# Two more late Q tiles, additions for z tied to VectorE's normalises, and a new list of steps

## The chip, the cores and the metric

The kernel runs on one core of a Trainium2 chip. The metric is the device time of one execution in microseconds; before the change it is 510.95 us, the median of three runs (510.87 to 511.24).

## The reference

One block of a transformer on 2048 tokens of width 576, in bfloat16. A layernorm feeds two branches in parallel, linear attention with 32 heads of 18, and a gated feed-forward of width 4608:

```python
def _A_ref(x, wqkv, wo):
    q, k, v = split_heads(x @ wqkv)
    phi = lambda t: jnp.where(t > 0, t + 1, jnp.exp(t)) + 1e-6
    pq, pk = phi(q), phi(k)
    kv = jnp.einsum("bhsd,bhse->bhde", pk, v)
    z = jnp.einsum("bhsd->bhd", pk)
    num = jnp.einsum("bhqd,bhde->bhqe", pq, kv)
    den = jnp.einsum("bhqd,bhd->bhq", pq, z)[..., None] + 1e-6
    return merge_heads(num / den) @ wo
def _B_ref(x, w_gate, w_up, w_down):
    return (_gelu(x @ w_gate) * (x @ w_up)) @ w_down
xn = _layernorm(x)
return x + _A_ref(xn, A_wqkv, A_wo) + _B_ref(xn, B_w_gate, B_w_up, B_w_down)
```

## The kernel before

The tokens are 16 tiles (n = 0 to 15) of 128. There is a head, which does the layernorm and gathers the attention's sums, and then four groups (sc = 0 to 3) of four tiles each, which do the feed-forward and the output.

**The head.** For each tile: statistics of two halves and their aggregate on VectorE (L226, L229); the reciprocal deviation as a logarithm and an exponential on ScalarE (L233, L234); the normalised tile `xn`, on VectorE (L247) where the string NORM has a D for the tile, on ScalarE (L242) where it has an A, and then GpSimd first makes its bias (L237); the transposed copy `xnT`, by TensorE and copies (L268, L272) for tiles 0 and 1, by a DMA transpose that SyncE issues (L275) for the others. K is multiplied in two halves of 288 columns with five matmuls each (L283), one PSUM bank for each half, so a half can't be multiplied for the next tile until phi has read this tile's. Phi is an exponential on ScalarE (L298) and a maximum on VectorE (L303). Q goes the same way through two other banks. G = xn^T phi(k) is accumulated in PSUM over the tiles (L322, seven matmuls a tile now, two more a tile at the head's end, and a strip, L329); V is multiplied in only afterwards (L402). The sum z of phi(k) over the tiles is added up on GpSimd, one addition of 128 x 576 a tile from tile 1 on (L212), and read by a matmul near the head's end (L390).

**Late Q.** The tiles in LATE have no Q in the head. Their Q is computed at the start of the group they lie in, in front of its gate/up (`late_q`, with the class `_LateQ`): per tile ten and then eight matmuls on 64 rows, which take two row tiles of TensorE in turn (L353, the line that gate/up's matmuls have too), then an exponential (L714), a minimum (L715) and a maximum with an addition (L716) for each of two halves. Two such tiles are held at a time, with two banks each, out of a ring of eight that the gate/up units and the output tiles use as well. Before, group 1 has late tiles 6 and 7, group 2 has 9, 10 and 11, group 3 has 13, 14 and 15, and group 0 none.

**The groups.** Gate/up: 18 pairs of units of 18 half-row matmuls with 512 columns for each of two F tiles (L353, 648 matmuls a group), gelu on ScalarE (L694), product on VectorE (L695). Then down and the attention's part for the four tiles (L800, L805), the sum with x (L814), and the store. Weights are loaded by SyncE as buffers come free.

**What sets the order.** In the head every piece of work is a step with an engine, a planned cost, a rank and the steps that it comes after. The order in which the steps are emitted, and so the order on each engine's queue, is written out in the text HEAD; a step that HEAD lacks would be placed by the planner `in_order` behind it. Engines take their instructions strictly in this order, and wait by semaphores for the data and buffers that they need. The letters: x load of x, s statistics, a aggregate, r reciprocal deviation, b bias on GpSimd, n normalise, t transpose on TensorE, c the copy or DMA into `xnT`, m multiply, e exponential, p phi, z addition for z, G accumulation of G, w five idle matmuls, B mask, g clearing of buffers. The numbers are tile, then 1 for K or 0 for Q, then half. The planned costs and tails (`took`, `tail`, `ready`) have no effect while HEAD names every step. A step's `after` alone makes no semaphore: it only orders.

Of the kernel before, what the change touches and what calls it, by code (L numbers as in the profile page):

```python
# [43 lines left out]
LATE = (6, 7, 9, 10, 11, 13, 14, 15)  # L44
# [16 lines left out]
def kernel(  # L61
# [149 lines left out]
    def z_add(n):
        nc.gpsimd.tensor_tensor(  # L212
            out=z_bf[:] if n == NS - 1 else z_sum[:], in0=pk[:, 0, PK0:PK0 + D] if n == 1 else z_sum[:], in1=pk[:, n, PK0:PK0 + D],
            op=ALU.add,
        )

# [29 lines left out]
    def ln_norm(n, c0=0, c1=D):  # L246
        nc.vector.tensor_scalar(  # L247
# [91 lines left out]
    SYNC = mybir.DependencyInfo(mybir.DependencyClass.Sync, mybir.DependencyReason.DATA)  # L339
# [130 lines left out]
    for n0 in range(8, NS, 2):  # L470
        step(("x", n0), "SP", 1.30, n0 - 5.5, [], lambda n0=n0: load_x(n0, 2), ready=1.6 * n0 + 2.0, tail=3.0)
    for n in range(NS):
        lead = LEAD[n] if n < 4 else 0.0
        after_x = [("x", n // 2 * 2)] if n >= 8 else []
# [58 lines left out]
    def in_order(steps):  # L533
# [351 lines left out]
```

## Time and profile before

| | before |
|---|---|
| median of three runs | 510.95 us |
| span of the profiled execution | 509.1 us |
| TensorE busy | 504.4 us, 4553 matmuls |
| VectorE, ScalarE, GpSimd busy | 215.7, 143.3, 26.6 us |
| head, until the first gate/up matmul | 56.6 us |
| last K multiply of the head ends | 46.6 us |
| addition for z on GpSimd (L212) | 1.29 us mean |
| DMA transpose (L275) | 1.21 us of issue, 2.6 us to landing (median) |

The profile is one execution. The busy share tells which engine is full; the chain of waits is followed back from the last instruction, and names at each piece what was being waited for; the timeline has every instruction with its start, its length and, in brackets, how long its engine had stood in front of it and what released it. A TensorE that is busy says nothing of the pace of its matmuls; the starts of successive ones do.

### The profile page before, as it was taken

Reading aid. Unit: us, or ns where it says so; the run is one execution under the profiler, and the core shown is the slowest. Engines: PE = TensorE matmul, PEld = TensorE weight load, DVE = VectorE, ACT = ScalarE, POOL = GpSimd, SP = SyncE. Lnnn points to the kernel's source line nnn. Section 1 sums busy time; section 2 is a strip of 40 time slices with the busy share of each in tenths; the row PEclk is TensorE's granted clock in tenths of the full one; section 3 lists DMA queues with packets and bytes.
Section 4 is the critical chain, followed back from the end, with each engine's and each line's share of the span. In section 5 each row is a group of like instructions: output and inputs, shape, how many; then the busy total and the mean of one; then the engine's idle time right before and its main releaser. Section 6 shows DMA issues by size and latency. Waiting matters only on the chain.

```text
span 509.1 us, 10828 instructions
## 1 busy us (share of the span) xinstructions
PE 504.4 (99%) x4553; PEld 303.5 (60%) x4553; DVE 215.7 (42%) x465; ACT 143.3 (28%) x273; POOL 26.6 (5%) x40
## 2 busy tenths in 40 slices
PE   8999999999999999999999999999999999999997
PEld 7878644444877544444777544445777444445774
DVE  7994555555100465455000655554101556544101
ACT  6886233223300332333000423323000433232000
POOL 3556000000000000000000000000000000000000
PEclk9999999999999999999999999999999999999999
DMA  6556599999020455666000465576000565551000
GB/s 211 135 102 163 155 262 283 253 267 234 18 71 0 117 155 163 170 160 153 14 13 0 125 170 164 153 171 136 13 13 0 147 172 154 163 130 14 13 13 23
DMA packets 119850, 62.00 MB, mean 122 GB/s; under 512 B 25778, under 2 KB 119098, under 8 KB 119802
## 3 DMA queue, kind: packets, MB, share of 16 engines
q1 hardware_dynamic: 119658, 61.17, 46.6%
q8 instruction: 35, 0.57, 0.5%
q14 instruction: 13, 0.11, 0.1%
q10 hardware_dynamic: 144, 0.15, 0.1%
HBM read 53.60 MB, written 2.36 MB: 110 GB/s over the span
## 4 chain that ended last, share of the span: by engine, by line
PE 97%; DVE 1%; DMA 0%; ACT 0%; issue 0%
PE ps_all L353 57%; PE ps_all L800 28%; PE ps_all L283 5%; PE ps_all L805 3%; PE ps_all L322 3%; DMA x_sb<-in_A_x_dram 0%; PE ps_all L788 0%; PE ps_all L329 0%; DVE stats L226 0%; DVE xn L247 0%; PE ps_all L402 0%; PE ps_all L291 0%; PE ps_all L740 0%; PE ps_all L268 0%; ACT phi_e L298 0%
## 5 line engine op out<-in xcount | busy, mean ns | idle before, releaser
L353 PE MATMUL ps_all<-xnT,wg 64*128 64x512 bf16 x1152 | 272.1, 376 | 0.0
L353 PE MATMUL ps_all<-xnT,wu 64*128 64x512 bf16 x1152 | 271.6, 376 | 0.0
L695 DVE TENSOR_TENSOR hT<-ps_all,gl 128x512 bf16<-128x512 f32 x144 | 99.6, 692 | 125.9 <-ACT gl L694 125.8
L353 PEld LDWEIGHTS <-wu 64*128 64x128 bf16 x1152 | 108.3, 94 | 68.0
L353 PEld LDWEIGHTS <-wg 64*128 64x128 bf16 x1152 | 108.3, 94 | 67.6
L800 PE MATMUL ps_all<-wd_sb,hT 128*128 128x288 bf16 (+2 forms) x1152 | 147.1, 286 | 0.0
L694 ACT ACTIVATE gl<-ps_all 128x512 f32<-128x512 f32 x144 | 86.0, 597 | 186.3 <-PE ps_all L353 186.1
L800 PEld LDWEIGHTS <-hT 128*128 128x128 bf16 x1152 | 110.9, 98 | 30.9 <-issue 1.2
L814 DVE TENSOR_TENSOR res<-ps_all,x_sb 128x288 bf16<-128x288 f32 (+2 forms) x32 | 13.8, 454 | 146.3 <-PE ps_all L805 88.1
L353 PE MATMUL ps_all<-xnT,wr 64*128 64x512 bf16 x288 | 54.7, 376 | 0.0
L714 ACT ACTIVATE gl<-ps_all 128x288 f32<-128x288 f32 x16 | 5.9, 410 | 119.0 <-PE ps_all L353 117.8
L283 PE MATMUL ps_all<-wqkv_sb,xnT 128*128 128x288 bf16 x230 | 30.9, 286 | 0.5 <-DVE hT L303 0.4
L283 PEld LDWEIGHTS <-xnT 128*128 128x128 bf16 x230 | 21.8, 97 | 6.0 <-issue 0.6
L298 ACT ACTIVATE phi_e<-ps_all,neg 128x288 f32<-128x288 f32 x48 | 23.1, 496 | 4.8 <-PE ps_all L283 2.0
L353 PEld LDWEIGHTS <-wr 64*128 64x128 bf16 x288 | 14.0, 94 | 16.7
L805 PE MATMUL ps_all<-m_sb,pqT 128*128 128x288 bf16 (+2 forms) x128 | 20.9, 286 | 0.0
L322 PE MATMUL ps_all<-hT,xn 128*128 128x288 bf16 (+4 forms) x144 | 18.4, 273 | 0.0
L212 POOL TENSOR_TENSOR z_sum<-z_sum,hT 128x576 f32<-128x576 f32 x13 | 16.8, 1289 | 1.9 <-DVE hT L303 1.4
L303 DVE SCALAR_TENSOR_TENSOR hT<-phi_e,ps_all 128x288 bf16<-128x288 f32 x32 | 14.1, 444 | 5.4 <-ACT phi_e L298 4.9
L322 PEld LDWEIGHTS <-xn 128*128 128x128 bf16 x144 | 13.8, 97 | 3.5 <-issue 0.2
L805 PEld LDWEIGHTS <-pqT 128*128 128x128 bf16 x128 | 12.4, 98 | 3.3
L226 DVE BATCH_NORM_STATS2 stats<-x_sb 128x6 f32<-128x288 bf16 x32 | 13.7, 448 | 1.1 <-DMA x_sb<-in_A_x_dram 1.1
(76 smaller groups left out, 171.5 us busy)
## 6 DMA issues: line engine op xcount, KB each, us to landing
wg<-in_B_w_gate_dram SPq DMA_DIRECT2D x72, 256.0 KB, 3.0
wu<-in_B_w_up_dram SPq DMA_DIRECT2D x72, 256.0 KB, 3.5
wd_sb<-in_B_w_down_dram SPq DMA_DIRECT2D x12, 432.0 KB, 5.1
wr<-in_B_w_gate_dram SPq DMA_DIRECT2D x72, 32.0 KB, 2.7
wr<-in_B_w_up_dram SPq DMA_DIRECT2D x72, 32.0 KB, 3.1
out_dram<-res SPq DMA_DIRECT2D x15, 144.0 KB, 2.0
wqkv_sb<-in_A_wqkv_dram SPq DMA_DIRECT2D x2, 576.0 KB, 4.8
x_sb<-in_A_x_dram SPq DMA_DIRECT2D x4, 288.0 KB, 3.3
```

Source lines behind the costliest of these rows:

```text
L212: nc.gpsimd.tensor_tensor(out=z_bf[:] if n == NS - 1 else z_sum[:], in0=pk[:, 0, PK0:PK0 + D] if n == 1 else z_sum[:], in1=pk[:, n, PK0:PK ...
L226: nc.vector.bn_stats(out=ln_raw[n][:, h, :], in_=x_sb[:, n, h * HALF:(h + 1) * HALF])
L283: nc.tensor.matmul(ps_all[:, KQ_BANK[which] + hf, :HALF], lhsT=xnT[:, kt, n * P:(n + 1) * P], rhs=wqkv_sb[:, kt, c:c + HALF], start=(kt == ...
L298: nc.scalar.activation(out=e[:], in_=ps_all[:, KQ_BANK[which] + hf, :HALF], func=ACT.Exp, bias=neg1[:], scale=1.0,)
L303: nc.vector.scalar_tensor_tensor(out=(pq, pk)[which][:, n, PK0 * which + hf * HALF:PK0 * which + (hf + 1) * HALF], in0=e_tiles[n, which, h ...
L322: nc.tensor.matmul(ps_all[:, b, col:col + w], lhsT=xn[:, n, kt * P:(kt + 1) * P], rhs=pk[:, n, PK0 + d0:PK0 + d0 + w], start=(n == 0 and c ...
L353: return nc.tensor.matmul(self.outs[i], lhsT=self.lhs(i, rows, kt), rhs=self.rhs(i, rows, kt), start=start, stop=stop, skip_group_check=True,)
L694: nc.scalar.activation(out=gl[:], in_=ps_all[:, b[0], :], func=ACT.Gelu_apprx_tanh)
L695: nc.vector.tensor_tensor(out=hT[:, GUB * k + i, :], in0=ps_all[:, b[1], :], in1=gl[:], op=ALU.mult)
L800: nc.tensor.matmul(self.acc(hf), lhsT=hT[:, f, j * P:(j + 1) * P], rhs=wd_sb[:, f, self.parts[hf]], start=(f == 0 and not paired), stop=Fa ...
L805: nc.tensor.matmul(self.acc(hf), lhsT=pqT[:, c, self.ts], rhs=m_sb[:, c, self.parts[hf]], start=False, stop=(paired and c == 3), skip_grou ...
L814: nc.vector.tensor_tensor(out=self.res[:, hs], in0=self.acc(hf), in1=x_sb[:, self.n, hs], op=ALU.add)
```

## The change

- LATE has ten tiles: 5 and 12 are new. So Q of tiles 0, 1, 2, 3, 4 and 8 stays in the head; group 1 has three late tiles and group 3 four.
- Each addition for z gets a real wait, on the end of a normalise of VectorE: that of the first tile at least four ahead which VectorE normalises, or the last such tile (14). It is meant to keep GpSimd's additions away from VectorE's normalises.
- x of tiles 8 to 15 is loaded with two DMAs of four tiles instead of four of two.
- The planner's costs and due times for these are adapted, and HEAD is a new list.

```diff
--- before.py
+++ after.py
@@ -41,7 +41,7 @@
 XW = 640
 KLO = HP + 1
 Q_CUT = 3
-LATE = (6, 7, 9, 10, 11, 13, 14, 15)
+LATE = (5,6,7,9,10,11,12,13,14,15)
 PK0 = 4
 PKW = D + 2 * PK0
 
@@ -205,14 +205,17 @@
         nc.gpsimd.memset(kvT[HP:P, 4, :], 0.0)
         nc.gpsimd.memset(ones[:], 1.0)
 
+    SYNC = mybir.DependencyInfo(mybir.DependencyClass.Sync, mybir.DependencyReason.DATA)
+    dve_norm = {}
     z_sum = apool.tile([P, D], F32, name="z_sum")
     z_bf = apool.tile([P, D], BF16, name="z_bf")
 
-    def z_add(n):
-        nc.gpsimd.tensor_tensor(
+    def z_add(n, norm):
+        z = nc.gpsimd.tensor_tensor(
             out=z_bf[:] if n == NS - 1 else z_sum[:], in0=pk[:, 0, PK0:PK0 + D] if n == 1 else z_sum[:], in1=pk[:, n, PK0:PK0 + D],
             op=ALU.add,
         )
+        tc.add_manual_dep(z.ins, dve_norm[norm].ins.name, SYNC, reason="out of the way of VectorE's normalise")
 
     mv = persist.tile([P, NS, nc.vector.BN_AGGR_DIM], F32, name="mv")
     rstd = persist.tile([P, NS], F32, name="rstd")
@@ -244,7 +247,7 @@
         )
 
     def ln_norm(n, c0=0, c1=D):
-        nc.vector.tensor_scalar(
+        dve_norm[n] = nc.vector.tensor_scalar(
             out=xn[:, n, c0:c1], in0=x_sb[:, n, c0:c1], scalar1=mv[:, n, 0:1], scalar2=rstd[:, n:n + 1],
             op0=ALU.subtract, op1=ALU.mult,
         )
@@ -336,7 +339,6 @@
 
 
     LO, HI = slice(0, HP), slice(HP, P)
-    SYNC = mybir.DependencyInfo(mybir.DependencyClass.Sync, mybir.DependencyReason.DATA)
     banks = _Ring([4, 5, 6, 7, 2, 3, 0, 1])
 
     class _Unit:
@@ -462,16 +464,18 @@
 
     GL = 0.0
     NORM = "DDDADADADADADADA"
+    Z_BEHIND = [min([m for m in range(n + 4, NS) if NORM[m] == "D"] or [NORM.rindex("D")]) for n in range(NS)]
     COPY = ("DVE", "ACT")
     LEAD = (-9.0, 0.5, -0.5, -0.5)
     X_AT = [3.35, 4.40, 6.30, 8.80] + [10.40] * 4
     W_AT = {1: 5.60, 0: (7.65, 8.45)}
 
-    for n0 in range(8, NS, 2):
-        step(("x", n0), "SP", 1.30, n0 - 5.5, [], lambda n0=n0: load_x(n0, 2), ready=1.6 * n0 + 2.0, tail=3.0)
+    X_LATE = {8: 9.70, 12: 13.30}
+    for n0, at in X_LATE.items():
+        step(("x", n0), "SP", 1.40, n0 / 4 + 0.5, [], lambda n0=n0: load_x(n0, 4), ready=at, tail=3.0)
     for n in range(NS):
         lead = LEAD[n] if n < 4 else 0.0
-        after_x = [("x", n // 2 * 2)] if n >= 8 else []
+        after_x = [("x", n // 4 * 4)] if n >= 8 else []
         x_at = X_AT[n] if n < 8 else 0.0
         for h in range(2):
             step(("stats", n, h), "DVE", 0.40, n - 2.2 + lead, after_x, lambda n=n, h=h: ln_half(n, h), ready=x_at, tail=0.02)
@@ -500,8 +504,9 @@
                 step(("bias", n), "POOL", 0.15, n - 2.1, [("rstd", n)], lambda n=n: ln_bias(n))
                 step(("norm", n), "ACT", 0.77, n - 2.1, [("bias", n)], lambda n=n: ln_norm_act(n), tail=0.09)
             else:
-                step(("norm", n), "DVE", 0.36, n - 2.1, [("rstd", n)], lambda n=n: ln_norm(n), tail=0.07)
-            step(("xnT", n), "SP", 1.25, n - 1.9, [("norm", n)], lambda n=n: dma_transposes(n), tail=2.9 if n < 4 else 2.0)
+                quiet = [("z", m) for m in range(1, n) if Z_BEHIND[m] < n][-1:]
+                step(("norm", n), "DVE", 0.36, n - 2.1, [("rstd", n)] + quiet, lambda n=n: ln_norm(n), tail=0.07)
+            step(("xnT", n), "SP", 1.25, n - 1.9, [("norm", n)], lambda n=n: dma_transposes(n), tail=1.6)
             ready = [("xnT", n)]
         for which, rank in ((1, n), (0, n + 0.6))[:1 if n in LATE else 2]:
             for h in range(2):
@@ -520,9 +525,9 @@
                 step(("phi", n, which, h), "DVE", 0.37, r + 0.15, [("exp", n, which, h)],
                      lambda n=n, w=which, h=h: kq_phi(n, w, h), tail=0.08)
         if n > 0:
-            idle = [("bias" if NORM[n + 4] == "A" else "norm", n + 4)] if n + 4 < NS else []
+            idle = [("norm", Z_BEHIND[n])]
             step(("z", n), "POOL", 1.40, n + 2.0, [("phi", m, 1, h) for m in (0, n) for h in range(2)] + idle + ([("z", n - 1)] if n > 1 else []),
-                 lambda n=n: z_add(n))
+                 lambda n=n: z_add(n, Z_BEHIND[n]))
         clear = [] if n else [("xnT", m, i) for m in range(TD) for i in range(2)]
         step(("G", n), "PE", 0.75, n + 1.15, [("phi", n, 1, 0), ("phi", n, 1, 1)] + clear, lambda n=n: g_accumulate(n, G_A))
     step(("spin",), "PE", 0.30, -1.0, [("tp", 0, 1)], lambda: spin(5))
@@ -549,22 +554,21 @@
         return [name for _, _, name in sorted(begun)]
 
     HEAD = """
-        s0.1 s0.0 a0 s1.0 r0 n0.0 n0.1 t0.0 t0.1 s1.1 a1 c0.1 c0.0 w s2.0 m0.1.0 s2.1 r1 a2 r2 n1.0 e0.1.0 n1.1
-        m0.1.1 t1.0 n2 p0.1.0 t1.1 m0.0.0 c1.0 m0.0.1 c1.1 s3.0 s3.1 e0.1.1 p0.1.1 B m1.1.0 a3 e0.0.1 m1.1.1 p0.0.1
-        e0.0.0 s4.0 r3 p0.0.0 e1.1.0 G0 s4.1 b3 n3 m1.0.1 e1.1.1 g a4 r4 c2 e1.0.1 m1.0.0 p1.1.0 s5.1 p1.1.1 s5.0
-        m2.1.0 e1.0.0 n4 p1.0.1 m2.1.1 G1 p1.0.0 m2.0.1 e2.1.0 a5 e2.1.1 p2.1.0 r5 p2.1.1 c3 s6.0 c4 m2.0.0 s6.1
-        e2.0.1 b5 a6 G2 e2.0.0 x8 p2.0.0 m3.1.0 p2.0.1 m3.1.1 s7.0 n5 c5 e3.1.0 e3.1.1 m3.0.1 s7.1 r6 p3.1.0 z1
-        m3.0.0 m4.1.0 e3.0.1 p3.1.1 m4.1.1 e3.0.0 a7 G3 n6 e4.1.0 s9.0 x10 r7 p3.0.0 z2 s9.1 m4.0.0 p4.1.0 m5.1.0
-        e4.1.1 a9 p4.1.1 b7 s8.0 z3 p3.0.1 n7 m5.1.1 s8.1 e5.1.0 G4 r9 e5.1.1 p5.1.0 c6 a8 e4.0.0 s11.0 m4.0.1 r8
-        m6.1.0 e4.0.1 p5.1.1 m6.1.1 s10.1 p4.0.0 n8 b9 s11.1 e6.1.0 e6.1.1 p6.1.0 G5 n9 m5.0.0 x12 p6.1.1 e5.0.0 a11
-        p4.0.1 c7 m7.1.0 m7.1.1 z4 s10.0 s13.0 e7.1.0 e7.1.1 a10 G6 c8 x14 m5.0.1 p7.1.0 p7.1.1 r10 r11 s13.1 p5.0.0
-        n10 s12.1 z5 m8.1.1 s12.0 e5.0.1 a13 b11 m8.1.0 z6 e8.1.1 c9 e8.1.0 c10 p8.1.1 a12 n11 G7 p8.1.0 r12 p5.0.1
-        m8.0.0 s14.0 m9.1.1 m9.1.0 G8 r13 n12 e9.1.1 z7 b13 e9.1.0 p9.1.1 s14.1 c11 m8.0.1 n13 p9.1.0 m10.1.1 s15.0
-        s15.1 e8.0.0 e10.1.1 m10.1.0 a14 z8 p10.1.1 G9 a15 m11.1.1 e10.1.0 p10.1.0 r14 e8.0.1 p8.0.0 e11.1.1 r15 c12
-        m11.1.0 p8.0.1 p11.1.1 c13 n14 e11.1.0 z9 m12.0.0 c14 b15 n15 m12.0.1 m12.1.1 p11.1.0 e12.1.1 p12.1.1
-        m12.1.0 e12.1.0 p12.1.0 e12.0.0 G10 m13.1.1 c15 e13.1.1 m13.1.0 p12.0.0 e13.1.0 G11 z10 p13.1.1 m14.1.1
-        p13.1.0 e12.0.1 e14.1.1 z11 p14.1.1 m14.1.0 e14.1.0 p14.1.0 G13 m15.1.1 e15.1.1 p12.0.1 z12 m15.1.0 e15.1.0
-        G14 p15.1.1 p15.1.0 G12 G15
+        s0.0 s0.1 a0 s1.1 r0 n0.0 t0.0 n0.1 c0.0 s1.0 a1 t0.1 c0.1 r1 m0.1.0 s2.0 s2.1 m0.1.1 a2 e0.1.0 n1.1 r2 t1.1
+        n1.0 c1.1 m0.0.0 p0.1.0 t1.0 e0.1.1 m0.0.1 c1.0 n2 e0.0.1 s3.0 s3.1 p0.1.1 a3 w e0.0.0 r3 c2 s4.1 m1.1.0
+        p0.0.0 s4.0 e1.1.0 p0.0.1 G0 p1.1.0 b3 m1.1.1 a4 n3 s5.0 e1.1.1 m1.0.0 x8 r4 m1.0.1 m2.1.0 p1.1.1 c3 s5.1
+        m2.1.1 e1.0.0 a5 e1.0.1 G1 p1.0.0 e2.1.0 n4 e2.1.1 m2.0.0 r5 p1.0.1 p2.1.0 s6.0 b5 m2.0.1 p2.1.1 m3.1.0
+        m3.1.1 G2 s7.0 s6.1 n5 s7.1 e3.1.0 p3.1.0 c4 a6 e3.1.1 m4.1.0 p3.1.1 e2.0.0 a7 r6 m4.1.1 c5 p2.0.0 s8.1
+        e4.1.0 r7 m3.0.0 n6 c6 G3 e4.1.1 p4.1.0 m5.1.0 s8.0 b7 e2.0.1 p4.1.1 s9.0 s9.1 a8 m5.1.1 n7 p2.0.1 e5.1.0 a9
+        e5.1.1 e3.0.0 x12 p5.1.0 r9 p5.1.1 G4 m3.0.1 z1 z2 m6.1.0 c7 r8 m6.1.1 s11.0 p3.0.0 e6.1.0 e6.1.1 n8 s11.1
+        b9 p6.1.0 g p6.1.1 s10.0 m4.0.0 n9 z3 G5 m7.1.0 s10.1 e3.0.1 a10 e7.1.0 c8 s12.0 B z4 m7.1.1 p7.1.0 G6
+        e7.1.1 c9 m8.1.0 a11 p7.1.1 m8.1.1 p3.0.1 r10 s13.0 n10 m4.0.1 e4.0.0 e8.1.0 r11 c10 e8.1.1 b11 p8.1.0
+        p4.0.0 e4.0.1 z5 n11 p8.1.1 s12.1 a12 G7 m9.1.0 m9.1.1 s13.1 m8.0.0 p4.0.1 m8.0.1 z6 e9.1.0 e9.1.1 p9.1.0
+        a13 m10.1.0 p9.1.1 s14.1 r12 r13 m10.1.1 n12 e10.1.0 c11 s15.0 c12 G9 e10.1.1 p10.1.0 b13 p10.1.1 s15.1 z7
+        s14.0 m11.1.0 a14 m11.1.1 n13 c13 e11.1.0 e11.1.1 p11.1.0 z8 a15 p11.1.1 G10 m12.1.0 r14 r15 m12.1.1 e12.1.0
+        e12.1.1 n14 b15 G11 p12.1.0 n15 m13.1.0 p12.1.1 e13.1.0 m13.1.1 c14 p13.1.0 e13.1.1 G12 p13.1.1 e8.0.1 z9
+        m14.1.0 z10 c15 p8.0.1 m14.1.1 G8 e14.1.0 e14.1.1 p14.1.0 m15.1.0 p14.1.1 m15.1.1 G14 z11 z12 G13 e8.0.0 z13
+        e15.1.0 p8.0.0 z14 e15.1.1 p15.1.0 p15.1.1 z15
     """
     KIND = {
         "x": "x", "s": "stats", "a": "aggr", "r": "rstd", "b": "bias", "n": "norm", "t": "tp", "c": "xnT", "m": "mm",
```

## The prediction

> **What bounds the kernel now.** Steps go by the list's short names: `m1.1.0` is the multiply of tile 1, K (the middle 1; 0 is Q), half 0; `e`, `p` its exponential and phi; `s a r b n` the layernorm; `c` the transpose; `G`, `z` the accumulations. I read the page's busy times first:
>
> ```profile
> PE 504.4 (99%) x4553; PEld 303.5 (60%) x4553; DVE 215.7 (42%) x465; ACT 143.3 (28%) x273; POOL 26.6 (5%) x40
> ```
>
> TensorE is busy for all but 4.7 us of 509.1, so an edit can only pay by taking TensorE work away or by closing one of few gaps. Then the chain of waits (start, length, what), for where those gaps are:
>
> ```profile
> 6.27 1.40 PE ps_all L283 x10
> 8.11 1.23 PE ps_all L291 x10
> 9.33 1.30 PE ps_all L283 x10
> ...
> 28.02 0.51 ACT phi_e L298
> 29.73 1.39 DVE xn L247
> 31.13 0.73 DVE stats L226 x2
> 32.33 1.39 PE ps_all L283 x10
> ...
> 46.64 5.72 PE ps_all L322 x49
> ...
> 56.70 70.28 PE ps_all L353 x652
> ...
> 167.88 72.14 PE ps_all L353 x684
> 279.92 73.24 PE ps_all L353 x702
> ...
> 393.06 73.24 PE ps_all L353 x702
> ```
>
> From 6.27 on the chain is TensorE, piece joined to piece, with one excursion to VectorE at 29.73 to 32.33. The two lower groups price a late Q tile: 684, 702 and 702 matmuls are the 648 of gate/up and 2, 3 and 3 times 18. One late tile more is 73.24 - 72.14 = 1.10 us. In the head a Q tile is ten matmuls of 1.23 us (the second line). The timeline (start, length, engine, line) shows the excursion:
>
> ```profile
> 29.65 1.48 DVE L247 TENSOR_SCALAR xn<-x_sb,mv,rstd 128x576 bf16<-128x576 bf16 x1
> 29.68 2.64 POOL L212 TENSOR_TENSOR z_sum<-z_sum,hT 128x576 f32<-128x576 f32 x2
> ...
> 31.15 0.77 PE L283 MATMUL ps_all<-wqkv_sb,xnT 128*128 128x288 bf16 x5
> ...
> 32.33 1.39 PE L283 MATMUL ps_all<-wqkv_sb,xnT 128*128 128x288 bf16 x10 [0.40 <-DVE hT L303]
> ```
>
> The normalise of tile 10 takes 1.48 us beside an addition for z of 1.3 us; the median of L247 is 0.41. The phi behind it comes late, and TensorE, done with five matmuls at 31.15 + 5 x 0.123 = 31.77, stands until 32.33: 0.56 us.
>
> **What the Trainium skill says.** "SBUF — State Buffer", section "SBUF: two separate sides", says that VectorE and GpSimd share one port pair, held exclusively for a whole instruction, so that a VectorE instruction in a two-port mode blocks until the GpSimd one ends. The 1.48 us agree: 0.41 plus most of one 1.29 us addition. "TensorEngine Tiling (Array Packing)", section "Key Properties", says that row tiles run in parallel; the trace agrees, since 18 half-row matmuls take 1.10 us, the time of nine full ones. "DMA: Bandwidth & Descriptors", section "Queues, rings and completion order", says that DMAs of one issuer share rings, in order, but may finish out of it. Here a transpose lands after 2.6 us (median), and the one issued at 25.12, with an x load of 288 KB issued at 26.38, took 4.0.
>
> **The change part by part.** *Two Q tiles leave the head* (5 and 12; tile 5 joins 6 and 7 in group 1, tile 12 joins 13 to 15 in group 3). TensorE: -2 x 1.23 = -2.46 us. VectorE loses 4 phi and ScalarE 4 exponentials, worth nothing by themselves.
>
> *Two late Q tiles are added*: +2 x 1.10 = +2.20. Behind them queues gate/up, so all of it is on the path. The group of four needs a look. VectorE paces its ends at 0.71 us a half (L715 of the last group at 395.26, 395.98, 396.69). Its first phi ends at 396.06, so the banks of the second late tile are free at 396.06 + 3 x 0.71 = 398.19. Gate/up's second unit wants them at 392.89 + 4 x 1.10 + 1.07 = 398.36 (1.07 for ten row matmuls with 512 columns, two at a time). That is 0.17 us of room; bounds 2.20 to 2.5, and I take 2.20.
>
> *The additions wait for a normalise.* Each z waits for the next VectorE normalise at least four tiles ahead; behind it on GpSimd stand `b11`, `b13` and `b15`, for which ScalarE's normalise and then a transpose wait. This removes the 0.56 us. For its cost I walk the list below. The last z: seven additions from about n14 on, 7 x 1.29 = 9 us, or p15 plus 1.28 us, ends before 47; the matmul that reads it came at 56.03 and will come near 53. Free.
>
> *x in two loads.* `x8` stands in front of `c3`, `x12` behind `c6`. x8 is issued about 9.7 and, at the 4.2 us of the present four-tile load, is there at 13.9; the first statistics that read it are due at 18.7. x12: 20.7 + 4.2 = 24.9, needed at 26.4. Free as data.
>
> *The new list.* I add along each engine's list with the pitches of this timeline: statistics 0.365 us a half (two from 17.11 to 17.84), aggregate 0.12, normalise on VectorE 0.33, phi 0.37 (two from 16.37 to 17.11), exponential 0.435 (four from 12.66 to 14.40), rstd 0.42, normalise on ScalarE 0.78, an addition 1.29; a waiting engine begins about 0.05 to 0.1 us after its releaser. Per tile without Q: TensorE 1.23 + 0.75 = 1.98; VectorE 0.73 + 0.12 + 0.74, and 0.33 on every other tile, mean 1.76; ScalarE 0.87 + 0.42, and 0.78 on every other, mean 1.68. So TensorE is still the slowest, by 0.2 us. Points of the walk:
> - Start. The first multiply stays at 6.27: the VectorE chain before it is the same. `e0.1.0` now goes ahead of `r2`, and `r2`, `c1.1`, `e0.1.1`, `c1.0` follow on ScalarE. `c1.0` also waits for `t1.0`, now behind `m0.0.0`. It ends about 9.45, so `m1.1.0` begins near 9.55, where it was 9.33. TensorE's work in front ends at 6.27 + 1.23 + 0.43 + 1.23 = 9.16: a gap of 0.39 us against 0.17 now. The five idle matmuls `w` lie in it.
> - `c3` issued near 12.05, due at 15.97; `c6` 19.5, due 23.15; `c9` 25.9, due 30.3; `c14` 37.6, due 40.7; `c15` 39.6, due 42.7. At 2.6 us each is in time, by 0.5 to 1.8 us.
> - Banks. A K half is multiplied again after the other half and a G, 0.615 + 0.75 = 1.37 us, in which exp and phi must end. The trace has this loop:
>
> ```profile
> 42.12 1.50 ACT L298 ACTIVATE phi_e<-ps_all,neg 128x288 f32<-128x288 f32 x3 [0.47 <-PE ps_all L283]
> ...
> 42.66 0.46 DVE L303 SCALAR_TENSOR_TENSOR hT<-phi_e,ps_all 128x288 bf16<-128x288 f32 x1 [0.52 <-ACT phi_e L298]
> ...
> 43.28 1.39 PE L283 MATMUL ps_all<-wqkv_sb,xnT 128*128 128x288 bf16 x10
> ```
>
>   The multiply ended at 42.09 and the phi at 43.12: 1.03 us of 1.37. In my walk the tightest are `m4.1.0`, `m11.1.0`, `m12.1.0` and `m13.1.0`, each with about 0.25 us left. None breaks.
> - Normalises against GpSimd: n10 at 28.8 behind z4 (until 28.1), n12 near 33 behind z6 (31.8), n14 near 37.5 behind z8. Only the clearing `g` may meet n8, some 0.4 us, with 0.9 in hand.
>
> Sum of the head to the last K multiply: before, 24 x 1.23 + 0.43 + 13 x 0.75 = 39.70, plus gaps 0.17 and 0.56, from 6.27: 46.70 (the chain has 46.64). After, 22 x 1.23 + 0.43 + 9.75 = 37.24 plus 0.39: 43.90. So -2.74. What follows in the head (two or three G, the G_B row, strips, key-value product) has the same matmuls; the weights' issues on SyncE begin after `c15`, about 40.8 against 41.63, and the first gate/up block then lands near 49 for a start at 54. Net -2.74 + 2.20 = -0.54: 510.95 - 0.54 = 510.4.
>
> **The rivals.**
> - *Larger x loads hold up the transposes.* For: the 4.0 us above, with half as many bytes behind it. Against: the transpose issued at 19.24, also with a load 1.26 us behind it, took 3.0. If 576 KB cost twice the 1.4 us excess, `c2` (issued 8.5, due 12.76, 1.66 to spare) stalls TensorE by 1.1 us, and `c6` (1.05 to spare) by 1.75: 2.9 in all. Half of that: 510.4 + 1.45 = 511.9, slower than before.
> - *Without Q there is nothing to fill waits.* Q multiplies can run while K's banks are drained; some ten tiles now have none. If the in-order queues of VectorE and ScalarE cost each 0.1 us over the 0.25 of room, it is ten times 0.1: 511.4; at 0.2 it is 512.4. I put it at 511.6. For: VectorE is busy for 4.4 to 5.0 of each 5 us from 5 to 35. Against: two Q fewer relieve just these queues, by 1.5 and 1.7 us.
> - *No gap at the start, and a late tile that overlaps more than I count*: -0.39 and some 0.1 for each: 509.9. The profile gives little for it; everything before 8 us seems set by x and the copies.
>
> **How the numbers follow.** My sum 0.58, held transposes 0.17, exposed waits 0.15, the better start 0.10. The predicted time is the first, 510.4. 0.2% is 1.02 us: faster means under 509.93, slower over 511.97. All of the first case but 0.03 lies within; the fourth is split, 0.07 faster; of the second and third a little over half lies beyond 511.97: 0.18. So faster 0.10, same 0.72, slower 0.18. The range of 509.8 to 512.0 leaves out some 0.05 below and 0.15 above.
>
> **What would show it.** The chain should have the last K multiply end near 43.9 and gate/up begin near 54.0; no L247 above 0.8 us; groups of 684 + 18 = 702, 702 and 720 matmuls of 73.2, 73.2 and 74.3 us. The held transposes would show as landings over 3.7 us and idle time of L283 at `m2` or `m6`; exposed waits as many small idle pieces in front of L283, released by VectorE's phi. Wrong would be a head that ends later than 55, or a group of four over 74.7 us.

## The result and the profile after

The changed kernel takes 513.53 us (median of six runs, 512.0 to 515.11) where the kernel before takes 510.95 (510.79 to 511.24). The ratio is 1.0053, with a 95% interval of 1.0033 to 1.0073: slower by about 2.6 us. Predicted were 510.4 us and a range of 509.8 to 512.0, so the time lies outside the range and on the side that had 0.18. The runs of the changed kernel also scatter over 3 us, those of the kernel before over 0.5.

The busy times of the profiled execution after the change (span 511.5 us):

```profile
PE 505.9 (99%) x4569; PEld 304.1 (59%) x4569; DVE 216.6 (42%) x469; ACT 143.3 (28%) x273; POOL 26.4 (5%) x40
```

TensorE got 16 matmuls more, 36 for two late tiles less 20 for two Q tiles of the head, and is busy for 1.5 us more. The predicted sum has less work on it: -2.46 + 2.20 = -0.26. So the loss is not only idle time: about 1.8 us of it are matmuls that took longer. The chain of waits (start, length, what) says which:

```profile
6.51 2.58 PE ps_all L286 x10
...
9.31 1.06 PE ps_all L294 x6
...
11.07 0.51 ACT phi_e L301
...
11.62 0.44 PE ps_all L142 x5
12.06 0.61 PE ps_all L286 x5
12.67 0.75 PE ps_all L325 x7
...
23.79 4.59 DMA xnT<-xn
...
28.43 1.40 PE ps_all L286 x10
...
46.70 5.73 PE ps_all L325 x49
...
56.76 70.28 PE ps_all L355 x652
...
167.94 73.24 PE ps_all L355 x702
...
281.08 73.24 PE ps_all L355 x702
...
394.22 74.34 PE ps_all L355 x720
```

The three lower groups are as predicted to the hundredth: 702, 702 and 720 matmuls in 73.24, 73.24 and 74.34 us, 2.20 more than before. The head is not: its last K multiply ends at 46.70 instead of 43.90, and gate/up begins at 56.76, where 54.0 was predicted and the kernel before stands at 56.70. Three things are new in the chain. The first ten multiplies of K take 2.58 us instead of 1.40. From 10.58 the chain is on ScalarE, for a copy and then the exponential at 11.07, and the five idle matmuls `w` (L142) follow it. At 23.79 it leaves TensorE again, for a transpose that lands after 4.59 us. The start in the timeline of TensorE (start, length, engine, line, and in brackets the idle time ahead and its releaser):

```profile
5.44 0.72 PE L271 MATMUL ps_all<-ident,xn 128*128 128x128 bf16 x5 [0.47 <-DVE xn L250]
6.51 2.58 PE L286 MATMUL ps_all<-wqkv_sb,xnT 128*128 128x288 bf16 x10 [0.36 <-ACT xnT L275]
8.89 0.42 PE L271 MATMUL ps_all<-ident,xn 128*128 128x128 bf16 x2
...
11.62 0.44 PE L142 MATMUL ps_all<-warm 128*128 128x128 bf16 x5 [0.59 <-ACT phi_e L301]
```

The ten multiplies begin at 6.51 and the next instruction at 8.89, so they are 0.24 us apart here, against 0.123 for ten multiplies in 1.23 us: half the rate. The column of the granted clock stays at full speed in all of it; the half rate is to be read from the spacing alone. And `w`, which the new list puts behind the first Q multiplies, waits for the exponential of Q (half 1 of tile 0): both use bank 7, so `w` can't write before that exponential has read.

That bank has a second reader, which the new list leaves behind `w`: the phi of the same half, `p0.0.1`. In the timeline of VectorE it is the second of the two phis of Q of tile 0, and it begins after `w` has ended at 12.06:

```profile
12.73 0.44 DVE L306 SCALAR_TENSOR_TENSOR pq<-phi_e,ps_all 128x288 bf16<-128x288 f32 x1
```

So `w` has written zeros over 128 columns of Q of tile 0 before phi reads them. Phi takes the larger of the capped exponential and what stands in the bank, so in these columns it is wrong wherever Q is positive. The overwriting costs no time, but the place of `w` in the new list is a fault, not only a loss; e1 and f2 below don't have it, g3 does.

The second transpose of the chain in the timeline of SyncE (when it issued what):

```profile
23.12 0.57 SPq L96 DMA_DIRECT2D x_sb<-in_A_x_dram  x1
23.79 5.55 SPq L278 DMA_TRANSPOSE xnT<-xn  x3
```

The load `x12` of four tiles is issued at 23.12, and `c7` is the first of the three transposes behind it, 0.67 us later. The undisturbed transposes of this trace land after 2.6 us.

The normalise of VectorE that had taken 1.48 us beside an addition is gone from the list of its line (duration in ns, min/median/max):

```profile
L250 DVE TENSOR_SCALAR xn<-x_sb,mv,rstd x11: 275/415/582, 5.0 to 39.8; 128x576 bf16<-128x576 bf16 x7, 128x384 bf16<-128x384 bf16 x2, 128x192 bf16<-128x192 bf16 x2
```

The longest is 0.58 us: `n8`, against the clearing `g`.

### The profile page after: what moved, and what is told of

It is laid out like the page before. It is cut to its first block, busy times and chain, and to the rows that moved or that the text cites. A ratio compares the mean times of both kernels' runs of the same rounds, so it can differ in the third digit from the quotient of the medians.

```text
span 511.5 us, 10853 instructions
## 1 busy us (share of the span) xinstructions
PE 505.9 (99%) x4569; PEld 304.1 (59%) x4569; DVE 216.6 (42%) x469; ACT 143.3 (28%) x273; POOL 26.4 (5%) x40
## 4 chain that ended last, share of the span: by engine, by line
PE 97%; DMA 1%; ACT 0%; DVE 0%; issue 0%
PE ps_all L355 57%; PE ps_all L804 28%; PE ps_all L286 5%; PE ps_all L809 3%; PE ps_all L325 3%; DMA xnT<-xn 1%; DMA x_sb<-in_A_x_dram 0%; PE ps_all L792 0%; PE ps_all L332 0%; PE ps_all L404 0%; PE ps_all L294 0%; PE ps_all L744 0%; ACT xnT L275 0%; PE ps_all L271 0%; DVE stats L229 0%; ACT phi_e L301 0%
## 5 line engine op out<-in xcount | busy, mean ns | idle before, releaser
L718 ACT ACTIVATE gl<-ps_all 128x288 f32<-128x288 f32 x20 | 7.6, 410 | 120.2 <-PE ps_all L355 118.6
L286 PE MATMUL ps_all<-wqkv_sb,xnT 128*128 128x288 bf16 x210 | 29.4, 293 | 0.6 <-ACT xnT L275 0.4
L286 PEld LDWEIGHTS <-xnT 128*128 128x128 bf16 x210 | 20.3, 100 | 6.0 <-ACT xnT L275 0.6
L301 ACT ACTIVATE phi_e<-ps_all,neg 128x288 f32<-128x288 f32 x44 | 21.1, 498 | 6.4 <-PE ps_all L286 4.2
```

What stands on the lines that cost most here:

```text
L286: nc.tensor.matmul(ps_all[:, KQ_BANK[which] + hf, :HALF], lhsT=xnT[:, kt, n * P:(n + 1) * P], rhs=wqkv_sb[:, kt, c:c + HALF], start=(kt == ...
L301: nc.scalar.activation(out=e[:], in_=ps_all[:, KQ_BANK[which] + hf, :HALF], func=ACT.Exp, bias=neg1[:], scale=1.0,)
```

## The experiments

The theory: the head's new order is worth what was predicted, but the place of `w` and the loads of x take it back. `w` does so twice, by its wait and because nothing keeps TensorE busy in front of the first K multiply. Rivals: the new list itself is worse (exposed waits), the new waits of z cost, or the late tiles do. The times below are medians; the kernel before, run beside each, had medians of 510.81 to 510.97, and none of its 153 runs was above 511.56.

### One cause at a time, on the changed kernel

**e1_w_back**: `w` goes back in front of the first K multiply; the rest is the changed kernel.

```diff
-        s0.0 s0.1 a0 s1.1 r0 n0.0 t0.0 n0.1 c0.0 s1.0 a1 t0.1 c0.1 r1 m0.1.0 s2.0 s2.1 m0.1.1 a2 e0.1.0 n1.1 r2 t1.1
+        s0.0 s0.1 a0 s1.1 r0 n0.0 t0.0 n0.1 c0.0 s1.0 a1 t0.1 c0.1 r1 w m0.1.0 s2.0 s2.1 m0.1.1 a2 e0.1.0 n1.1 r2 t1.1
...
-        n1.0 c1.1 m0.0.0 p0.1.0 t1.0 e0.1.1 m0.0.1 c1.0 n2 e0.0.1 s3.0 s3.1 p0.1.1 a3 w e0.0.0 r3 c2 s4.1 m1.1.0
+        n1.0 c1.1 m0.0.0 p0.1.0 t1.0 e0.1.1 m0.0.1 c1.0 n2 e0.0.1 s3.0 s3.1 p0.1.1 a3 e0.0.0 r3 c2 s4.1 m1.1.0 p0.0.0
```

> The changed kernel with the five idle matmuls moved back in front of the first K multiply, nothing else. Clock theory (they keep TensorE busy while the copies run, and so bring it to full rate): ten matmuls of the first K multiply take 1.4 us instead of 2.58, tile 1's K starts near 9.6 instead of 12.06, and the time falls by about 2.4 us to 511, with the runs within 0.5 us of one another. Rival, the larger x loads: the loss is the transposes' wait; the time stays above 512.5.

Measured: 511.86 us (511.02 to 513.51, 20 runs), ratio 1.0020 [1.0013, 1.0027]. So 1.7 of the 2.6 us went with one step of the list, where 2.4 and runs within 0.5 us of one another were expected. `m1.1.0` begins at 9.40, and the ten K multiplies take 1.40. What is left is in the chain of waits of this kernel:

```profile
11.96 4.75 DMA xnT<-xn
...
16.77 1.40 PE ps_all L286 x10
...
22.27 4.72 DMA xnT<-xn
...
27.03 1.40 PE ps_all L286 x10
```

These are `c3`, issued 1.9 us behind the load `x8`, and `c7`, 0.66 us behind `x12`. TensorE stands 0.79 and 0.36 us for them, 1.15 together.

**f2_x_as_before**: e1 with x in four loads of two tiles again, behind `c4`, `c5`, `c6` and `c8`.

```diff
-    X_LATE = {8: 9.70, 12: 13.30}
-    for n0, at in X_LATE.items():
-        step(("x", n0), "SP", 1.40, n0 / 4 + 0.5, [], lambda n0=n0: load_x(n0, 4), ready=at, tail=3.0)
+    for n0 in range(8, NS, 2):
+        step(("x", n0), "SP", 1.30, n0 - 5.5, [], lambda n0=n0: load_x(n0, 2), ready=1.6 * n0 + 2.0, tail=3.0)
...
-        n5 s7.1 e3.1.0 p3.1.0 c4 a6 e3.1.1 m4.1.0 p3.1.1 e2.0.0 a7 r6 m4.1.1 c5 p2.0.0 s8.1
+        n5 s7.1 e3.1.0 p3.1.0 c4 x8 a6 e3.1.1 m4.1.0 p3.1.1 e2.0.0 a7 r6 m4.1.1 c5 x10 p2.0.0 s8.1 e4.1.0 r7 m3.0.0 n6
```

> The changed kernel with the idle matmuls back in front of the first K multiply, and x of tiles 8 to 15 in four loads of two tiles at the places that the kernel before has (behind c4, c5, c6 and c8). Transfer theory (a DMA transpose issued behind a load of four tiles lands after 4.2 to 4.8 us instead of 2.6, and stalled TensorE by 0.79 and 0.36 us at tiles 3 and 7 with the idle matmuls back): both stalls go, 511.86 - 1.15 = 510.7. Rival, that only the sum of bytes counts: the stalls move to other tiles and it stays within 0.3 of 511.86.

Measured: 510.39 us (510.10 to 511.07, 12 runs), ratio 0.9993 [0.9985, 1.0002]. Its chain of waits never leaves TensorE between 9.46 us and gate/up:

```profile
9.46 0.79 PE ps_all L286 x5
10.25 0.75 PE ps_all L325 x7
...
43.99 5.73 PE ps_all L325 x49
...
54.06 70.28 PE ps_all L355 x652
```

The last K multiply ends at 43.99 and gate/up begins at 54.06; 43.90 and 54.0 were predicted. The list, the late tiles and the waits of z together are worth what the prediction's sum gave them. **f2_again** is the same kernel once more, since the interval had held 1.

> The kernel of f2 once more, with more rounds, for its interval against the kernel before: 510.4, 0.4 us under it, and no run over 511.2 if the idle matmuls in front keep the clock up in every execution. Rival: slow runs by late transposes as in f3 and g5, median 510.7 or more.

Measured: 510.43 us (510.17 to 511.15, 13 runs), ratio 0.9990 [0.9982, 0.9998]. The interval now lies just below 1: about 0.5 us faster than the kernel before, and 3 us faster than the changed one.

**g3_w_late**: f2 with `w` in the changed kernel's place, the other cause alone.

```diff
-        s0.0 s0.1 a0 s1.1 r0 n0.0 t0.0 n0.1 c0.0 s1.0 a1 t0.1 c0.1 r1 w m0.1.0 s2.0 s2.1 m0.1.1 a2 e0.1.0 n1.1 r2 t1.1
-        n1.0 c1.1 m0.0.0 p0.1.0 t1.0 e0.1.1 m0.0.1 c1.0 n2 e0.0.1 s3.0 s3.1 p0.1.1 a3 e0.0.0 r3 c2 s4.1 m1.1.0 p0.0.0
+        s0.0 s0.1 a0 s1.1 r0 n0.0 t0.0 n0.1 c0.0 s1.0 a1 t0.1 c0.1 r1 m0.1.0 s2.0 s2.1 m0.1.1 a2 e0.1.0 n1.1 r2 t1.1
+        n1.0 c1.1 m0.0.0 p0.1.0 t1.0 e0.1.1 m0.0.1 c1.0 n2 e0.0.1 s3.0 s3.1 p0.1.1 a3 w e0.0.0 r3 c2 s4.1 m1.1.0
```

> The changed kernel with x as the kernel before loads it, and the five idle matmuls where the change puts them: behind the exponential of Q's second half of tile 0, whose bank they write (so that phi of these 128 columns reads zeros, as in the changed kernel). Place theory: they wait for that exponential and then run on the path, 0.95 us; 510.39 + 0.95 = 511.3 in the better runs, and runs some 1.5 us over that more often than in f2. Rival, that with x right the place costs nothing: 510.4.

Measured: 511.86 us (511.11 to 513.44, 20 runs), ratio 1.0019 [1.0012, 1.0026]. Fifteen runs lie from 511.11 to 512.23 and five from 513.09 up. The timeline of TensorE in an execution of 511.11 us:

```profile
6.36 1.40 PE L286 MATMUL ps_all<-wqkv_sb,xnT 128*128 128x288 bf16 x10 [0.39 <-ACT xnT L275]
...
9.89 0.44 PE L142 MATMUL ps_all<-warm 128*128 128x128 bf16 x5 [0.59 <-ACT phi_e L301]
```

Here K runs at full rate, and what is left is the wait of `w` alone: `m1.1.0` comes at 10.33 instead of 9.46, 0.87 us later.

With these, four kernels make a square that differs in two things only: neither 510.39 (f2), `w` behind Q 511.86 (g3), x in two loads 511.86 (e1), both 513.53 (the changed kernel). The place of `w` costs 1.47 us, the loads cost 1.47 us, and both together 3.14. The 0.2 us more than their sum mean nothing: the interval of the changed kernel's six runs is 1 us wide to either side.

### Why `w` costs more than its wait

**g4_w_bank2**: g3 with `w` writing bank 2, so that it waits for no exponential.

```diff
-    def spin(count):
+    def spin(count, bank=7):
...
-            nc.tensor.matmul(ps_all[:, 7, 0:P], lhsT=warm[:], rhs=warm[:], start=True, stop=True)
+            nc.tensor.matmul(ps_all[:, bank, 0:P], lhsT=warm[:], rhs=warm[:], start=True, stop=True)
...
-    step(("spin",), "PE", 0.30, -1.0, [("tp", 0, 1)], lambda: spin(5))
+    step(("spin",), "PE", 0.30, -1.0, [("tp", 0, 1)], lambda: spin(5, 2))
```

> The last kernel with the idle matmuls writing bank 2, which nothing holds at that time. Place theory: the wait for the exponential goes and they lie in TensorE's wait for the copy of tile 1; the better runs come at 510.5. If runs 1.5 us slower remain, they come from the clock at the start and not from this wait. Rival, that the bank has no part: as the last kernel.

Measured: 511.48 us in the median, ratio 1.0011 [1.0000, 1.0023], but in two groups: six runs from 510.28 to 511.0 and six from 511.96 to 512.85. The lower group lies within f2's range (510.10 to 511.07), and its median is 0.8 us under that of g3's lower fifteen, so the wait for the exponential is worth about what g3 shows. The chain of waits of an execution of 512.33 us shows what the upper group has:

```profile
6.60 2.58 PE ps_all L286 x10
...
11.33 0.28 PE ps_all L142 x5
11.61 0.61 PE ps_all L286 x5
```

No wait, but the half rate for the first ten multiplies. It costs 512.33 - 510.3 = 2.0 us. In the changed kernel's profile the last Q multiply of tile 0 ends at 11.03 (10.38 + 0.65 in the timeline) against 9.38 in f2's (8.73 + 0.65): 1.65 us for the half rate, and then 12.06 - 11.03 - 0.08 = 0.95 for the wait and `w`; 0.08 is f2's own gap there.

**g2_cold**: f2 with eight idle matmuls at the start instead of 35, and no `w` (left out: idle matmuls only).

```diff
-NWARM = 35
+NWARM = 8
...
-    step(("spin",), "PE", 0.30, -1.0, [("tp", 0, 1)], lambda: spin(5))
...
-        s0.0 s0.1 a0 s1.1 r0 n0.0 t0.0 n0.1 c0.0 s1.0 a1 t0.1 c0.1 r1 w m0.1.0 s2.0 s2.1 m0.1.1 a2 e0.1.0 n1.1 r2 t1.1
+        s0.0 s0.1 a0 s1.1 r0 n0.0 t0.0 n0.1 c0.0 s1.0 a1 t0.1 c0.1 r1 m0.1.0 s2.0 s2.1 m0.1.1 a2 e0.1.0 n1.1 r2 t1.1
```

> The kernel of f2 (idle matmuls in front, x in four loads) with 8 idle matmuls at the start instead of 35 and none in front of the first K multiply, so that TensorE has hardly run when the work begins. Clock theory: the first K multiply takes 2.58 us for ten matmuls as in the profile of the changed kernel, and so on for some 3 us; every run is 1.2 to 1.8 us over f2's 510.39: 511.6 to 512.2. Rival: the slow first matmuls of the changed kernel came from something else; 510.4.

Measured: 513.61 and 513.84 us (two runs), ratio 1.0053; 511.6 to 512.2 were expected. The timeline of TensorE:

```profile
1.05 1.04 PE L142 MATMUL ps_all<-warm 128*128 128x128 bf16 x8 [1.05 <-DVE x_sb L120]
5.53 0.72 PE L271 MATMUL ps_all<-ident,xn 128*128 128x128 bf16 x5 [3.44 <-DVE xn L250]
6.60 2.58 PE L286 MATMUL ps_all<-wqkv_sb,xnT 128*128 128x288 bf16 x10 [0.36 <-ACT xnT L275]
```

With few idle matmuls in front, the half rate is there, with the very 2.58 us of the changed kernel. (This execution also has a transpose that came late, 4.28 us, so that its 3.3 us over f2 are not the half rate alone.) Compare f2's start, in the same view:

```profile
5.36 0.72 PE L271 MATMUL ps_all<-ident,xn 128*128 128x128 bf16 x5 [0.39 <-DVE xn L250]
5.87 0.74 PE L142 MATMUL ps_all<-warm 128*128 128x128 bf16 x5
6.43 1.45 PE L286 MATMUL ps_all<-wqkv_sb,xnT 128*128 128x288 bf16 x10
```

The five transposes take 0.72 us in both, so f2's execution was at half rate at 5.36 too. `w` stands behind them, and the K multiplies behind `w` run at full rate but for the first. In the changed kernel TensorE stood idle for 0.36 us at this point, and the half rate went on. The Trainium skill's page "TensorE: Matmul & The Clock Gate", section "What's actually happening", describes such a thing: the array runs at half rate while idle and goes to full rate after a window of about 3.4 us in which it was busy, and that window runs freely. The traces agree with the factor of two (0.24 against 0.123 us). They also show a scatter such as a free window would give: at 5.4 us the transposes took 0.72 us in some executions (f2, the changed kernel) and 0.52 in another (g3). How much idle time a window tolerates no run shows. Here a gap of 0.36 us behind some 4.6 us of idle matmuls and transposes was enough in some executions, and not in others.

The traces of all runs, laid side by side, say more. All kernels but g2 start with 35 idle matmuls (38 in f3). In the ten that have `w` in front of K, the spacing is first that of the full rate between 4.2 and 7.1 us. Of the five without it there, three are at full rate by 6.6 us (e2, e3, g3), and two only at 10.0 and 10.4 (the changed kernel, g4); g2 is at 10.6. With one execution of each this is no rate of such starts, but 3.4 us before 10.0 and 10.4 are 6.6 and 7.0, inside the span of the others: it is what a window of that length, missed once, would look like. That it is the idle time in front of K which makes the window be missed is argued from this and from f2, g3 and g4; no run varies that time alone.

**f3_warm** meant to test this from the other side: f2 with more idle matmuls, 38 at the start and eight in `w`.

```diff
-NWARM = 35
+NWARM = 38
...
-    step(("spin",), "PE", 0.30, -1.0, [("tp", 0, 1)], lambda: spin(5))
+    step(("spin",), "PE", 0.30, -1.0, [("tp", 0, 1)], lambda: spin(8))
```

> The last kernel with 38 instead of 35 idle matmuls in front of the first transpose and 8 instead of 5 behind it, so that TensorE hardly stands before the first K multiply. Clock theory: the slow runs, 1.2 to 1.8 us over the others, which a quarter of the runs of the variants with the new list show, become rare or go; median 510.6. Rival, that they come from transfers: as many slow runs as without.

Measured: 511.65 us (510.62 to 513.61, 20 runs), ratio 1.0019 [1.0012, 1.0026]. This expectation was missed: it is slower than f2 by 1.26 us. In the profiled execution K runs at full rate, but a transpose lands late: `c8`, 4.76 us, and TensorE stands 1.3 us for it. So it says nothing against the half rate and nothing for it; it moved the times of the transposes.

**e2_before_no_w** and **e3_after_no_w** leave `w` out (idle matmuls only) of the kernel before and of the changed one.

```diff
-        s0.1 s0.0 a0 s1.0 r0 n0.0 n0.1 t0.0 t0.1 s1.1 a1 c0.1 c0.0 w s2.0 m0.1.0 s2.1 r1 a2 r2 n1.0 e0.1.0 n1.1
+        s0.1 s0.0 a0 s1.0 r0 n0.0 n0.1 t0.0 t0.1 s1.1 a1 c0.1 c0.0 s2.0 m0.1.0 s2.1 r1 a2 r2 n1.0 e0.1.0 n1.1
```

> The kernel before without its five idle matmuls. Clock theory: the first multiplies run at half rate, 1.2 to 2.5 us are lost, 512 to 513.5, and the runs scatter by over 1 us as those of the changed kernel do. Rival, that they only fill a wait: 511.0 within 0.2, no scatter.

> The changed kernel without any idle matmuls. The clock theory adds two costs: half rate at the start, about 1.6 us, which stays, and 0.95 us for the place of the idle matmuls, which wait for the exponential of Q (they write its bank) and then run on the path; only this goes: 512.6. Rival, that their place is all of it: 510.9.

Measured: before without `w` 511.15 us (510.79 to 512.75, 12 runs), ratio 1.0013 [1.0004, 1.0022], with eight runs up to 511.45 and four from 512.52 up. After without `w` 511.38 (510.87 to 514.12, 19 runs), ratio 1.0018 [1.0009, 1.0028], with six above 512.4. Neither expectation is met as it stood: 512 to 513.5 or a steady 511.0 for the first, 512.6 or 510.9 for the second. Both profiled executions are of the lower kind, with K at full rate. In e3's, `c3` took 4.2 and `c7` 4.55 us. The same step is struck out of both lists; the diff is that of before. That the upper runs are the half rate is argued, from g4's 2.0 us; there is no trace of one. It fits that of the 178 runs of the kernel before and of f2, which have `w` in front of K, none lies 1.5 us up. But e1 and f3 have it there too, and reach 513.51 and 513.61; whether these are late transposes or the half rate isn't shown.

### What the loads of x do

**b2_x4_only**: the kernel before with x in two loads of four tiles; on SyncE they stand behind `c4` and `c6`, where `x8` and `x12` of two tiles were.

```diff
-    for n0 in range(8, NS, 2):
-        step(("x", n0), "SP", 1.30, n0 - 5.5, [], lambda n0=n0: load_x(n0, 2), ready=1.6 * n0 + 2.0, tail=3.0)
+    for n0 in range(8, NS, 4):
+        step(("x", n0), "SP", 1.30, n0 - 5.5, [], lambda n0=n0: load_x(n0, 4), ready=1.6 * n0 + 2.0, tail=3.0)
```

> The kernel before with x of tiles 8 to 15 in two loads of four tiles, at the places of its loads of tiles 8 and 12 (behind c4 and c6), nothing else. Transfer theory: the transposes c5 and c7 behind them land 1.6 to 2.1 us later; c5 and c7 have up to 1 us in hand in the list of before, so 0.5 to 1.5 us are lost: 511.4 to 512.4. Rival: 510.9 within 0.2.

Measured: 510.90 us (510.77 to 511.12, 12 runs), ratio 1.0003 [0.9994, 1.0011]: no loss, where 511.4 to 512.4 were expected. So 576 KB at a time are harmless in the old list; `c5` took 2.9 and `c7`, 1.35 us behind a load, 3.5 us, and both were in time. In the changed list the load stands 0.66 us ahead of `c7`, whose reader comes soon.

**g5_x_spread**: f2 with the two-tile loads earlier, behind `c2`, `c4`, `c5` and `c6`, to have none near `c7` and `c8`.

```diff
-        n1.0 c1.1 m0.0.0 p0.1.0 t1.0 e0.1.1 m0.0.1 c1.0 n2 e0.0.1 s3.0 s3.1 p0.1.1 a3 e0.0.0 r3 c2 s4.1 m1.1.0 p0.0.0
+        n1.0 c1.1 m0.0.0 p0.1.0 t1.0 e0.1.1 m0.0.1 c1.0 n2 e0.0.1 s3.0 s3.1 p0.1.1 a3 e0.0.0 r3 c2 x8 s4.1 m1.1.0
...
```

> The kernel of f2 with the four loads of two tiles behind c2, c4, c5 and c6, so that no load stands behind c8, which landed after 3.3 to 4.8 us with one behind it. Transfer theory: c8 lands after 2.6 to 3.4 us in every run; median 510.3 and no run over 511. Rival, that the loads only move the trouble to c3 or c7: 510.7 or more.

Measured: 511.71 us (511.47 to 512.68, 17 runs), ratio 1.0017 [1.0010, 1.0024]. Missed. The chain of waits shows `c8`:

```profile
22.89 1.66 PE ps_all L286 x14
24.55 4.61 DMA xnT<-xn
29.21 2.01 PE ps_all L286 x15
```

TensorE stands about 1.1 us for it, and the last load of x had been issued 3.5 us before it.

**h1_x_burst**: e1 with both four-tile loads in front of `c2`, the extreme of it.

```diff
-        n1.0 c1.1 m0.0.0 p0.1.0 t1.0 e0.1.1 m0.0.1 c1.0 n2 e0.0.1 s3.0 s3.1 p0.1.1 a3 e0.0.0 r3 c2 s4.1 m1.1.0 p0.0.0
+        n1.0 c1.1 m0.0.0 p0.1.0 t1.0 e0.1.1 m0.0.1 c1.0 n2 e0.0.1 s3.0 s3.1 p0.1.1 a3 e0.0.0 r3 x8 x12 c2 s4.1 m1.1.0
...
```

> The changed kernel with the idle matmuls in front and both loads of four tiles issued ahead of c2, so that no load of x stands near c3 to c15. If loads of x are what makes c3, c7 and c8 late, these three land after 2.6 to 3.0 us; c2, now behind both loads, lands near 13.5 and costs up to 1 us at tile 2. If c8 still takes over 4 us in some profile, something else than loads of x makes it late.

Measured: 514.10 us (512.73 to 515.51, 4 runs), ratio 1.0053 [1.0038, 1.0068]. The chain of waits:

```profile
8.71 7.34 DMA xnT<-xn
16.09 1.40 PE ps_all L286 x10
```

The transpose behind the two loads takes 7.34 us, and TensorE stands 2.8 us for it, where up to 1 us was expected: a transpose does wait behind loads issued ahead of it. `c4` to `c7`, with no load near, are back at 2.6 us (the landing of `c3` isn't in the trace). But `c8` takes 4.8 us, and TensorE stands another 1.35 us until it lands. So there are two things. A load just ahead holds a transpose up; `c7` shows this best, with 2.6 us here, 3.3 to 3.5 in the kernels with 288 KB issued 0.66 us ahead of it, and 4.55 to 4.72 with 576 KB (e1, e3, the changed kernel). And `c8` is late in some kernels for another cause, which stays open.

One candidate for it was not tested. The DMA view shows transfers of a kind that it calls instruction, of 16 and 8 KB. At least one begins between issue and landing of `c8` in all sixteen traces, and both do wherever it took 4 us or more; but both do in five traces too in which it took 3.2 to 3.4 (f2 is one). None begins while `c7` is under way in e1, e3 and the changed kernel, so what the load does there stands without it. While `c3` is under way in e1 and e3 one does, so its 4.2 to 4.75 us may not be the load's alone.

### The other parts, on the kernel before

**e4_late_only**: ten late tiles in the list of before, with the steps of Q for tiles 5 and 12 struck out.

```diff
-LATE = (6, 7, 9, 10, 11, 13, 14, 15)
+LATE = (5, 6, 7, 9, 10, 11, 12, 13, 14, 15)
...
```

> The kernel before with tiles 5 and 12 made late and their Q steps taken out of the list, whose order stays. By the prediction's terms: head -2.46, late groups +2.20, so 510.7. Rival, exposed waits (without Q nothing fills the drain of K's banks): several stalls of 0.1 to 0.3 us in front of the K multiplies of tiles 5 to 13, 511.4 or more.

Measured: 513.26 us (513.06 to 513.44, 4 runs), ratio 1.0046 [1.0031, 1.0061]. Gate/up begins at 56.56, only 0.14 earlier than before, so of the 2.46 us of the two Q tiles 2.3 are lost again. The chain of waits has the longest stop in front of 29.93:

```profile
29.82 0.12 DVE mv L229
29.93 1.38 PE ps_all L283 x10
```

It names VectorE's aggregate, but no K multiply reads that. The list of waits (total, times, longest; PEld is TensorE's weight load) has two waits that end there, and one more:

```profile
PEld L283 <- DMA xnT<-xn: 2.0, 1, 2.0
PE ps_all L283 <- DVE mv L229: 1.8, 1, 1.8
PE ps_all L283 <- DVE hT L303: 0.5, 1, 0.5
```

The weight load is that of tile 8: `c8` was issued at 25.1 and landed 4.8 us later, at 29.9, when TensorE went on. So 1.8 us are the wait for a late transpose, and 0.5, at 38.9, is one for a phi. The Q multiplies had filled this time: in the kernel before TensorE came to tile 8 as `c8` landed. So the rival of the exposed waits is real in the old list, though less by drained banks than by a transpose. In the new list there is no such wait (f2). In these runs late tiles pay only with the new list.

**b3_z_only**: the kernel before with the waits of z alone; `z1` and `z3` stand behind the normalises they wait for.

```diff
-                 lambda n=n: z_add(n))
+                 lambda n=n: z_add(n, Z_BEHIND[n]))
...
```

> The kernel before with each addition for z waiting for its normalise, and with z1 put behind n6 and z3 behind n8 and b9 so that the order allows it. By the prediction: the normalise of tile 10 no longer takes 1.48 us, TensorE's stall of 0.56 us goes, 510.4. Rival: the additions delay b11 or b13 and with them a transpose; 511 or more.

Measured: 512.75 us (512.74 to 512.79, 4 runs), ratio 1.0039 [1.0024, 1.0054], where 510.4 was expected and 511 or more the rival. The chain of waits:

```profile
29.95 0.35 DVE xn L251
...
30.44 1.29 POOL z_sum L215
31.73 0.25 POOL nbias L241
32.01 0.87 ACT xn L246
```

An addition waits for a normalise of VectorE; behind it in GpSimd's queue stands the bias of the next normalise of ScalarE, and that chain repeats at 33.90 and 39.94. It costs 512.75 - 510.81 = 1.94 us. In the new list the biases have room: f2 has these waits too, and none on its chain.

## Why the prediction was wrong

**Right: the late tiles.** 1.10 us each and no stop of the group of four for banks: 73.24, 73.24, 74.34.

**Right: the walk of the new list**, as f2 shows: 43.99 and 54.06 measured, with 510.39 and 510.43 us for 510.4. That the total agrees to 0.03 us is partly luck: f3 and g5, which differ from f2 by six idle matmuls or by the places of the loads, lie 1.3 us higher with `c8` late, a wait that the walk doesn't have. The 0.56 us of the long normalise are gone, and the clearing `g` meets `n8` for less than the 0.4 us allowed for (0.58 instead of 0.41). The rival of missing Q work was rightly put below the sum. But in the old list (e4) 2.3 of the 2.46 us are lost to waits that the missing Q exposes, so the -2.46 belong to Q and the list together, not to Q alone.

**Right only in this list: z is free.** The queue behind it that the prediction named (`b11`, `b13`, `b15`) is what costs 1.94 us in the old list.

**Wrong: "The five idle matmuls `w` lie in it."** This is the first step that failed. `w` was taken as a filler without a releaser. It shares bank 7 with Q and waits for Q's exponential (and overwrites what Q's phi has yet to read), and then runs on the path: `m1.1.0` at 12.06, predicted 9.55. f2, with `w` in front, has 9.46. Of these 2.60 us, 0.95 are the wait and `w`. The other 1.65 are a second thing that the step left out: `w` in its old place filled the idle time in front of the first K multiply, and without it TensorE can stay at half rate to about 10 us. "The first multiply stays at 6.27" was near (6.51), but its length was taken over from before. By medians the place of `w` costs 1.47 us (g3 against f2).

**Wrong: "At 2.6 us each is in time."** This is the second. The 2.6 us are a median, of transposes that mostly have no load just ahead of them; in the trace before, `c6`, 0.85 us behind a load of 288 KB, took 3.0. The list puts `x8` in front of `c3` and `x12` in front of `c7`; there they took 4.2 to 4.75 us (e1, e3). In the changed kernel's own trace only `c7` is waited for, for 0.24 us, since everything else came later. By medians this is 1.47 us (e1 against f2). The rival of the held transposes named the mechanism, its size (1.45 us for 511.9, and e1 took 511.86) and the sign (landings above 3.7 us). But it looked at `c2` and `c6`, which have a load behind them, while it is the transpose behind the load that suffers; so that the size agrees is luck. Its evidence, the 4.0 us of the transpose issued at 25.12, was `c8`, which is late elsewhere with no load near. It was a rival for a share of 0.17, and it came together with the other one, which was not on the list.

The medians add up: 510.4 for the list, 1.47 and 1.47 for the two causes make 513.3, and 513.53 was measured. The shares in one execution can be quite others: in the trace of the changed kernel, which starts at half rate, the first multiply of tile 1 is 2.60 us behind f2's and the last K multiply 2.71, so the loads add 0.1 there. How often the changed kernel starts at half rate stays open: the one trace shown does, and five of its six runs lie above 513.2. In g3 only five of twenty lie above 513. Nor is it shown why e1 scatters up to 513.5; the upper runs have no trace.

## What to carry to other kernels

An instruction that does nothing for the result still has a place: before moving one, ask what it waits for (here a bank), what it overwrites, and what it was keeping busy. When a list of steps is moved as a whole, read durations for a step from a neighbour with the same things issued just ahead of it: a transpose behind a load is another transpose. And take such a change apart again afterwards; here the new list with the late tiles and the waits of z is worth 0.5 us, once two of its edits are left out.

## What the runs showed of the hardware that was not expected

- Half rate at the start comes and goes between executions with the same steps in front: ten 128x288 matmuls took 2.58 or 1.40 us in g4 and g3, with the granted clock shown as full in both. It costs 1.65 to 2.0 us here. With five idle matmuls (eight in f3) in the gap of 0.36 us in front of K, none of ten traces has it in more than the first three K multiplies, and no run of the kernel before or of f2 is as late as it would make it.
- A transpose of 2.6 us took 3.3 to 3.5 behind a load of 288 KB issued 0.66 us before, 4.5 to 4.7 behind one of 576 KB at that distance, 4.2 to 4.75 at 1.9 us, and 7.34 behind two of 576 KB. At 1.35 us behind 576 KB another took 3.5, so the distance alone doesn't give the figure.
- One transpose, `c8`, landed after 3.2 to 4.8 us in kernels that differ little around it; in g5 and h1, with no load issued within 3 us of it, it took 4.6 and 4.8. The cause is open.
